# Attention and MLP blocks on one core: residual sums and row statistics moved between engines, another order of the first tiles and of the early weights

## The chip, the cores and the metric

The program runs on one core of a Trainium2 chip, in one launch that holds all four blocks. The metric is the time of one execution on the device in microseconds (us); it is given as a median over executions, with the lowest and the highest.

A core has five engines, each with a queue of its own that is worked off in order: TensorE (PE in the profile; its weight loads are shown apart as PEld), VectorE (DVE), ScalarE (ACT), GpSimd (POOL) and SyncE (SP), which in this kernel issues all the DMAs. Engines wait for each other through semaphores.

## The reference

Two blocks of two kinds alternate: attention, MLP, attention, MLP, over the same rows `x` of 2048 tokens by 576 values, in bfloat16. Before each block the rows are normalized, and each block's output is added to its input. The weights are the same in both rounds.

```python
def _A_ref(x, wqkv, wo):                      # linear attention, 32 heads of 18
    q, k, v = split(x @ wqkv)
    phi = lambda t: jnp.where(t > 0, t + 1, jnp.exp(t)) + 1e-6
    pq, pk = phi(q), phi(k)
    kv = jnp.einsum("bhsd,bhse->bhde", pk, v)
    z = jnp.einsum("bhsd->bhd", pk)
    num = jnp.einsum("bhqd,bhde->bhqe", pq, kv)
    den = jnp.einsum("bhqd,bhd->bhq", pq, z)[..., None] + 1e-6
    return (num / den) @ wo

def _B_ref(x, w1, b1, w2, b2):                # MLP, inner width 4608
    y = _layernorm(x, axis=-1)
    h = _gelu(y @ w1 + b1)
    return h @ w2 + b2

x = x + _A_ref(_layernorm(x), wqkv, wo)
x = x + _B_ref(_layernorm(x), w1, b1, w2, b2)
x = x + _A_ref(_layernorm(x), wqkv, wo)
x = x + _B_ref(_layernorm(x), w1, b1, w2, b2)
```

The MLP normalizes rows that were normalized already. The kernel does both at once: from the variance of a row it forms `u` = var * (1 + eps) + eps^2, and the row is scaled by u^-0.5.

## The kernel before

**Tiles.** The tokens form 16 tiles of 128 rows (tile `t`), one row to a partition, and 4 chunks of 512 tokens (chunk `c`). The 576 columns are split into five blocks of 128 (`KD`), the last of which is half full, or into two halves of 288. The 32 heads lie in five groups `g` of up to seven.

**An attention layer** (`layer_A`) has two stages. In the *key stage* each tile is normalized, turned (transposed into `yT`), and multiplied by the key weights in two halves (`k_half`, L461: half 0 and half 1 of tile t are k(t,0) and k(t,1) below). ScalarE forms an exponential and a shifted copy from each PSUM result, VectorE joins them (`phi_parts`, L393, L396, L400, L404). Then `ky_acc` (L491) accumulates the product of `pk` with the normalized rows over all 16 tiles. Query projections (`q_proj`, L502, 20 of them in a layer, one for each group and chunk) are strewn among the tiles: `q_at` says how many follow each tile, and a list `q_left` gives them out in order. Values need no pass over the tokens: `kv_ps` (L558) multiplies the accumulated product by the value weights, and `kv_wo` (L575) multiplies that by the output weights.

In the *output projection* the denominators of a chunk come from `den_stage` (L590, L598, L600), and `scale_stage` (L606, L608, L609) spreads them over the head columns on TensorE, copies them with ScalarE (`rden_bc`) and multiplies `pq` by them on VectorE. `wo_stage` (L617) then makes the 128x576 output of one tile, in one of two pairs of PSUM banks that take turns: tile t+2 can start when the sum of tile t has been read out. While chunk c is multiplied, chunk c+1 is scaled. After it, `residual` adds the layer's input and stores the rows to DRAM (`x_d`, L448). For tiles 2 and 3 ScalarE copies the PSUM result (L439) and GpSimd adds (L440), for all others VectorE does it in one instruction (L442). The result tile `xn` has five buffers.

**The next norm.** The rows of tiles 0 to 3 go straight on into the MLP's first chunk. `LNPipe` works in steps, one at each `tick`: statistics on VectorE (L278, L279 for the two halves, L284, and `u` in L292), the power on GpSimd (L298), a product (L302), the normalization on GpSimd (L313), and a DMA transpose (L365). For later chunks the MLP loads the rows again from `x_d`.

**The start.** `first_tiles` writes out by hand the order of tiles 0 to 5 on VectorE and ScalarE (`chain_on` binds each instruction to the one before it on its engine). `stats` (L804), `power` (L809, L811 on VectorE, L813 on GpSimd) and `norm` make the normalized rows: tiles 0 to 3 are normalized by VectorE (L820), tiles 4 and 5 by GpSimd (L824, L826). `turn` transposes on TensorE (L836) and copies the result (L839 to L842). From tile 6 on rows come through `LNPipe`, with normalization on GpSimd and a DMA transpose.

**PSUM.** `bank` gives out single banks under two tags, `h` and `g`, of two buffers each, in turn by a counter; once `ky_acc` has taken both buffers of `g`, only `h` is left until the end of the key stage.

**DMA order.** All loads of the start are bound in one chain (`chained`). Later weights (`late_pieces`) are issued between tiles: `piece_count` says how many after which tile, and each is held back until GpSimd's latest normalization (`gate`). The next layer's input rows are fetched ahead of the output projection (`prefetch_xo`, L421).

The MLP (`LayerB`) has two stages per chunk, `h` = gelu of rows times w1 (L718, L714) and the product with w2 (L765), and is not touched.

Of the kernel before, what the change touches and what calls it, by code (L numbers as in the profile page):

```python
# [7 lines left out]
ACT = mybir.ActivationFunctionType  # L8
# [7 lines left out]
P = 128  # L16
# [15 lines left out]
C1 = 1.0 + 1e-6  # L32


def build(tc, A_x, A_wqkv, A_wo, B_w1, B_b1, B_w2, B_b2, out, dbg=None, n_layers=4):
    nc = tc.nc
    dbg = dbg or {}
    with ExitStack() as ctx:
# [5 lines left out]
        bank_turn = dict(n=0, both=True)  # L44
# [133 lines left out]
        load_x0(1)  # L178
        load_wqkv(1, 0)
        load_x0(2)  # L180
        load_wqkv(1, 1)
        load_x0(3)
# [45 lines left out]
        def bias_turn():  # L228
# [6 lines left out]
        late_pieces = [piece_b1_dma, lambda: load_wqkv(2), piece_wo, w1_left[0], w1_left[1], w1_left[2],  # L235
                       lambda: piece_tail(0), w1_left[3], w1_left[4], lambda: piece_tail(1)] + w1_left[5:] + \
                      [(lambda i=i: piece_w2(i)) for i in range(6)]
        piece_count = {4: 1, 5: 2, 6: 1, 7: 2, 8: 1, 9: 1, 12: 2, 14: 3}
# [6 lines left out]
        class LNPipe:  # L245
# [3 lines left out]
            def feed(self, xt, t, kind, norm_eng, evac_eng="dve", load_from=None, after=None, agg_after=None,  # L249
                     keep=False):  # L250
                xbar = evac_eng == "xbar"
                self.items.append(dict(stage=(0 if load_from is None else -1), xt=xt, t=t, kind=kind,
                                       norm=norm_eng, evac=evac_eng, load=load_from,
                                       after=after, xbar=xbar, agg_after=agg_after, keep=keep))
# [4 lines left out]
            def tick(self, transposes=1):  # L259
                for it in list(self.items):  # L260
# [7 lines left out]
                    if st == -1:  # L268
# [5 lines left out]
                        it["xt"] = xn  # L274
                    elif st == 0:
# [20 lines left out]
                    elif st == 1:  # L296
                        rstd = work.tile([P, 1], F32, name="ln_rstd", bufs=6)
                        nc.gpsimd.tensor_tensor(out=rstd[:], in0=it["u"][:], in1=neg_half[:], op=ALU.pow)  # L298
                        it["rstd"] = rstd
                    elif st == 2 and it["norm"] != "dve":  # L300
                        nmr = work.tile([P, 1], F32, name="ln_nmr", bufs=4)
                        nc.gpsimd.tensor_scalar(out=nmr[:], in0=it["mv"][:, 0:1], scalar1=-1.0,  # L302
                                                scalar2=it["rstd"][:, 0:1], op0=ALU.mult, op1=ALU.mult)
                        it["nmr"] = nmr
                    elif st in (2, 3):
                        y = y_ring[state["ycnt"] % NY]
                        state["ycnt"] += 1
# [125 lines left out]
        def residual(li, t, halves, on_pool=False):  # L433
            xo = xo_of.pop((li, t))
            last = (li == n_layers - 1)
            xn = work.tile([P, D], F32, name="xn", tag="xn", bufs=5)
            res = xn[:, 0:HALF].bitcast(BF16) if last else xn[:]
            if on_pool:
                nc.scalar.copy(out=res.rearrange("p (h n) -> p h n", h=2), in_=halves)  # L439
                nc.gpsimd.tensor_tensor(out=res, in0=res, in1=xo, op=ALU.add)  # L440
            else:
                total = nc.vector.tensor_tensor(out=res.rearrange("p (h n) -> p h n", h=2), in0=halves,  # L442
                                                in1=xo.rearrange("p (h n) -> p h n", h=2), op=ALU.add)
                dve_last["sum"] = total.ins.name
            if last:
                nc.sync.dma_start(out=out_f[t * P:(t + 1) * P, :], in_=res)
                return None
            nc.sync.dma_start(out=x_d[t], in_=xn[:])  # L448
            return xn

        def layer_A(li, next_kind, pre_a1=None, first_tiles=None):
# [62 lines left out]
            if li > 0:  # L514
                for t in range(3):
                    y_load(t)
                begin, q_at = 0, {t: 1 for t in range(14)}
            else:
                first_tiles(k_half, ky_acc)
                begin, q_at = 5, {t: 1 + (t in (12, 14)) for t in range(4, NT)}  # L520
                ky_acc(3, range(KD))
                q_proj(*q_left.pop(0))
            for t in range(begin, NT):
                if li > 0 and t + 3 < NT:
                    y_load(t + 3)
                k_proj(t, 0)
                if t in q_at and t >= 1:
                    ky_acc(t - 1, range(KD - 1))
                k_proj(t, 1)
                pre_a1(t)  # L530
                if t >= 1:
                    ky_acc(t - 1, (KD - 1,) if t in q_at else range(KD))
                for _ in range(q_at.get(t, 0)):
                    q_proj(*q_left.pop(0))
# [77 lines left out]
            def wo_stage(t):  # L612
                c, j = divmod(t, TPC)
                wp = ps_acc.tile([P, 2, 512], F32, name="wo_ps", tag=("accA", "accB")[t % 2])
                for half in range(2):
                    for g in range(G):
                        pe(nc.tensor.matmul(wp[:, half, 0:HALF], lhsT=pq[(g, c)][0:GR[g], j * P:(j + 1) * P],  # L617
                                              rhs=kvwo[g][0:GR[g], half * HALF:(half + 1) * HALF],
                                              start=(g == 0), stop=(g == G - 1)))
                xn = residual(li, t, wp[:, :, 0:HALF], on_pool=t in (2, 3))  # L620
                if xn is not None and next_kind == "B" and t < TPC:
                    lnp.feed(xn, t, "B", "pool", "xbar")
# [18 lines left out]
            late_phi(after=dve_last["kvwo"], act_after=act_last["kvwo"])  # L641
            for t in range(NT):
# [3 lines left out]
                wo_stage(t)  # L646
# [9 lines left out]
                if t == NT - 3:  # L656
                    warm_table(ACT.Gelu_apprx_tanh, act_last["copy"])
                lnp.tick()
# [129 lines left out]
        def first_tiles(k_half, ky_acc):  # L788
# [26 lines left out]
            def norm(t, engine):  # L815
# [3 lines left out]
                if engine == "dve":  # L819
                    dve(nc.vector.tensor_scalar(out=y[:, 0:D], in0=it["x"][:], scalar1=it["mv"][:, 0:1],  # L820
                                                scalar2=it["rstd"][:, 0:1], op0=ALU.subtract, op1=ALU.mult))
                else:
                    nmr = work.tile([P, 1], F32, name="ln_nmr", bufs=4)
                    nc.gpsimd.tensor_scalar(out=nmr[:], in0=it["mv"][:, 0:1], scalar1=-1.0,  # L824
                                            scalar2=it["rstd"][:, 0:1], op0=ALU.mult, op1=ALU.mult)
                    last = nc.gpsimd.tensor_scalar(out=y[:, 0:D], in0=it["x"][:], scalar1=it["rstd"][:, 0:1],  # L826
                                                   scalar2=nmr[:], op0=ALU.mult, op1=ALU.add)
                    pool_last["norm"] = last.ins.name
# [23 lines left out]
            norm(0, "dve")  # L852
# [4 lines left out]
            norm(1, "dve")  # L857
            stats(2, (1,))
            power(2)
            a00, d00 = k_half(0, 0)  # L860
            act(*a00())
            turn(1, False)("dve")
            a01, d01 = k_half(0, 1)
            act(*a01())
            norm(2, "dve")
            a10, d10 = k_half(1, 0)
            stats(3)
            turn(2, True)()
            power(3)
            both(d00())  # L870
            act(*a10())
            a11, d11 = k_half(1, 1)
            act(*a11())
            norm(3, "dve")
# [6 lines left out]
            both(d10())  # L881
# [4 lines left out]
            norm(4, "pool")  # L886
            a30, d30 = k_half(3, 0)
            act(*a30())
            both(d20())
            both(d21())  # L890
# [7 lines left out]
            norm(5, "pool")  # L898
            both(d30())
            both(d31())  # L900
# [21 lines left out]
        for _ in range(4):  # L922
            late_pieces.pop(0)()
# [85 lines left out]
```

## Time and profile before

| what | us |
|---|---|
| median of 3 runs | 772.43 (771.15 to 772.85) |
| profiled execution | 770.18 |
| its span, first to last instruction | 768.5 |
| first key matmul (L461) | 6.13 |
| value weights used (L558), first attention layer | 69.32 |
| first output-projection matmul (L617) | 79.00 |
| first MLP matmul (L718) | 106.17 |
| first key matmul of the second attention layer | 388.06 |
| its first output-projection matmul | 456.16 |
| first MLP matmul after it | 483.08 |

A busy share is an average over the span, and the stages differ. The chain of work that ended last, followed back from the last instruction, is 93% TensorE: w2 has 37% of the span, w1 36%, the projections of the two attention layers most of the rest. VectorE has 3% of it, DMA, GpSimd and ScalarE 1% each. In a row of a timeline stand the start, the length (of a merged run of instructions, x their number), the engine, the line, the output and the inputs; in brackets follows how long the engine had been idle and what released it. In a list of waits stand who waited for whom, the total, the number of times and the longest. In a table of stretches each engine has its busy time.

### The profile page before, as it was taken

The numbers are of one execution on the slowest core, as the hardware profiler recorded it, in microseconds if no ns is written. First come the engines' busy times: TensorE is split into PE (matmuls) and PEld (weight loads), VectorE is DVE, ScalarE is ACT, GpSimd is POOL, SyncE is SP. The second block draws the span as 40 slices with busy tenths as digits, with TensorE's granted clock in tenths as the row PEclk, the third lists the DMA queues.
The fourth block names the chain that finished last, engine by engine and source line by source line (L and its number), as shares of the span: only waits on it lengthen the run. The fifth ranks groups of instructions, "written<-read, shape, count | busy, mean of one in ns | idle before, by whom it ended". The sixth has DMA issues, their size and how long they took to land.

```text
span 768.5 us, 15502 instructions
## 1 busy us (share of the span) xinstructions
PE 755.3 (98%) x6402; PEld 480.4 (63%) x6410; DVE 247.3 (32%) x651; ACT 317.9 (41%) x705; POOL 124.0 (16%) x216
## 2 busy tenths in 40 slices
PE   8999899999999999999999999999999999999998
PEld 4766554675477457646776666447745764674476
DVE  7886952125013402301244589462000000000000
ACT  4667546304600750263056674560065026205600
POOL 3670511013000301200100005321010010011000
PEclk9999999999999999999999999999999999999999
DMA  8979584027113703400431039672100110011000
GB/s 246 216 193 334 149 257 96 28 77 148 35 48 97 142 1 81 126 8 17 133 87 47 9 105 262 212 168 71 49 16 2 32 62 1 25 32 39 2 28 20
DMA packets 82865, 71.13 MB, mean 93 GB/s; under 512 B 44970, under 2 KB 67434, under 8 KB 82794
## 3 DMA queue, kind: packets, MB, share of 16 engines
q1 hardware_dynamic: 82794, 70.14, 33.9%
q8 instruction: 50, 0.82, 0.4%
q14 instruction: 21, 0.17, 0.1%
HBM read 41.74 MB, written 18.87 MB: 79 GB/s over the span
## 4 chain that ended last, share of the span: by engine, by line
PE 93%; DVE 3%; DMA 1%; POOL 1%; issue 1%; ACT 1%; SPq 0%; DVEq 0%; POOLq 0%
PE m_ps L765 37%; PE h_ps L718 20%; PE hp_ps L718 16%; PE q_ps L502 5%; PE ky_ps L491 5%; PE k_ps L461 5%; PE wo_ps L617 4%; DVE pq L609 1%; PE rden_ps L606 1%; DMA x_d<-xn 1%; DMA x<-in_A_x_dram 1%; DVE xn L442 0%; PE kv_ps L558 0%; POOL xn L440 0%; DVE kvwo L580 0%
## 5 line engine op out<-in xcount | busy, mean ns | idle before, releaser
L765 PE MATMUL m_ps<-w_sb,hT 128*128 128x288 bf16 x2304 | 283.6, 286 | 0.0
L765 PEld LDWEIGHTS <-hT 128*128 128x128 bf16 x2304 | 224.8, 98 | 59.8 <-issue 3.4
L718 PEld LDWEIGHTS <-w_sb 64*128 64x128 bf16 x2304 | 124.4, 94 | 136.6 <-issue 1.9
L718 PE MATMUL hp_ps<-yT,w_sb 64*128 64x512 bf16 x1152 | 178.0, 376 | 0.0
L442 DVE TENSOR_TENSOR xn<-m_ps,x_ring 128x576 f32<-128x576 f32 (+1 forms) x32 | 24.2, 758 | 415.4 <-PE m_ps L765 415.4
L718 PE MATMUL h_ps<-yT,w_sb 64*128 64x512 bf16 x1152 | 147.9, 376 | 0.0
L723 ACT COPY relay_sb<-relay_sb 128x1 f32<-128x1 f32 x144 | 28.5, 198 | 264.9 <-PE h_ps L718 222.6
L714 ACT ACTIVATE hT<-h_ps,b1T 128x512 bf16<-128x512 f32 x144 | 91.0, 683 | 44.5 <-PE h_ps L718 44.5
L714 ACT ACTIVATE hT<-hp_ps,b1T 128x512 bf16<-128x512 f32 x144 | 91.1, 692 | 0.0
L426 POOL TENSOR_TENSOR x_ring<-x_ring,b_bc 128x576 f32<-128x576 f32 x32 | 40.7, 1275 | 245.8 <-DMA x_ring<-x_d 243.0
L298 POOL TENSOR_TENSOR ln_rstd<-ln_u,neg_half 128x1 f32<-128x1 f32 x58 | 32.4, 559 | 294.1 <-DVE ln_u L289 201.8
L718 PE MATMUL h_ps<-yT,w_tail 64*128 64x512 bf16 x144 | 54.1, 376 | 0.0
L718 PE MATMUL hp_ps<-yT,w_tail 64*128 64x512 bf16 x144 | 54.1, 376 | 0.0
L461 PE MATMUL k_ps<-wqkv_sb,yT 128*128 128x288 bf16 x320 | 49.2, 286 | 0.9 <-ACT phi_a L396 0.6
L491 PE MATMUL ky_ps<-pk,y_ring 128*128 128x192 bf16 (+5 forms) x318 | 48.7, 285 | 0.5 <-ACT phi_a L396 0.2
L502 PE MATMUL q_ps<-yT,wqkv_sb 128*126 128x512 bf16 (+1 forms) x200 | 48.9, 379 | 0.1
L617 PE MATMUL wo_ps<-kvwo,pq 126*128 126x288 bf16 (+1 forms) x320 | 44.1, 286 | 5.0 <-DVE pq L609 3.1
L393 ACT ACTIVATE phi_e<-k_ps 128x288 bf16<-128x288 f32 x64 | 26.5, 413 | 50.9 <-PE k_ps L461 50.6
L617 PEld LDWEIGHTS <-pq 126*128 126x128 bf16 (+1 forms) x320 | 30.1, 97 | 17.8 <-DVE pq L609 5.1
L461 PEld LDWEIGHTS <-yT 128*128 128x128 bf16 x320 | 30.8, 98 | 14.2 <-issue 1.9
L718 PEld LDWEIGHTS <-w_tail 64*128 64x128 bf16 x288 | 27.1, 94 | 17.1
L400 DVE TENSOR_SCALAR phi_e<-phi_e 128x288 bf16<-128x288 bf16 (+2 forms) x104 | 28.5, 274 | 27.1 <-ACT phi_e L393 26.7
(102 smaller groups left out, 482.7 us busy)
## 6 DMA issues: line engine op xcount, KB each, us to landing
x_ring<-x_d SPq DMA_DIRECT2D x66, 288.0 KB, 3.1
x_d<-xn SPq DMA_DIRECT2D x48, 288.0 KB, 2.6
w_sb<-in_B_w_dram SPq DMA_DIRECT2D x6, 864.0 KB, 10.2
w_sb<-in_B_w_dram SPq DMA_DIRECT2D x9, 512.0 KB, 4.8
x<-in_A_x_dram SPq DMA_DIRECT2D x16, 144.0 KB, 3.6
x_ring<-in_A_x_dram SPq DMA_DIRECT2D x16, 144.0 KB, 3.0
y_d<-y_ring SPq DMA_DIRECT2D x16, 144.0 KB, 1.8
y_ring<-y_d SPq DMA_DIRECT2D x16, 144.0 KB, 2.2
```

The costliest lines, as they stand in the source:

```text
L298: nc.gpsimd.tensor_tensor(out=rstd[:], in0=it["u"][:], in1=neg_half[:], op=ALU.pow)
L393: exp = nc.scalar.activation(out=e[0:rows, 0:n], in_=ps_ap, func=ACT.Exp)
L400: low = nc.vector.tensor_scalar(out=e[0:rows, 0:n], in0=e[0:rows, 0:n], scalar1=1.0, scalar2=1e-6, op0=ALU.min, op1=ALU.add)
L426: nc.gpsimd.tensor_tensor(out=xo, in0=xo, in1=b2_bc[:], op=ALU.add)
L461: pe(nc.tensor.matmul(kp[:, 0:HALF], lhsT=yT[:, k, tok], rhs=wqkv_sb[:, k, D + half * HALF: D + (half + 1) * HALF], start=(k == 0), stop=( ...
L491: pe(nc.tensor.matmul(ky[at // 512][:, at % 512:at % 512 + n], lhsT=y_of[t][:, c * P:(c + 1) * P], rhs=pk_tiles[t][:, d:d + n], start=(t = ...
L502: pe(nc.tensor.matmul(qp[0:GR[g], :], lhsT=wqkv_sb[:, k, GO[g]:GO[g] + GR[g]], rhs=yT[:, k, c * CA:(c + 1) * CA], start=(k == 0), stop=(k ...
L617: pe(nc.tensor.matmul(wp[:, half, 0:HALF], lhsT=pq[(g, c)][0:GR[g], j * P:(j + 1) * P], rhs=kvwo[g][0:GR[g], half * HALF:(half + 1) * HALF ...
L714: act_last["gelu"] = nc.scalar.activation(out=hT[f][:, 0:CB], in_=dst[n], func=ACT.Gelu_apprx_tanh, bias=b1T[:, f:f + 1], scale=1.0).ins.name
L718: mm = pe(nc.tensor.matmul(dst[n], lhsT=wt, rhs=mv, start=(seen[n] == 0), stop=(seen[n] == 8)))
L723: relay = nc.scalar.copy(out=relay_sb[:, 1:2], in_=relay_sb[:, 0:1])
L765: pe(nc.tensor.matmul(acc[:, half, 0:HALF], lhsT=hT[f][:, j * P:(j + 1) * P], rhs=w2_sb[:, f, half * HALF:(half + 1) * HALF], start=(f == ...
```

## The change

- **Residual sums.** `residual` has one form again: VectorE adds, for all tiles.
- **Statistics of the MLP's first four tiles.** A new kind, `stat="act"`: ScalarE passes twice over the 576 columns, Identity and Square, each with a running sum over the row; the first sum (scaled) is the second's bias, so that the second sum is the variance. The passes write their unused results into the tile's `y` buffer. `u` moves to GpSimd, and the product's factor takes in the other scale of the mean. These tiles are also handed on one step later: tile t-1 is fed after tile t's work.
- **A query projection** goes from the key stage to a place behind `kv_wo(4)`, ahead of the first output-projection tile. In the first layer tile 13 now has two behind it instead of tiles 12 and 14, in the second layer tile 13 has none.
- **First tiles.** Token tile 2 is loaded ahead of the first half of the key weights, tile 3 ahead of the second half. k(1,0) comes ahead of k(0,1); `power(2)` stands behind the copy of tile 1's transposes; the joins of `phi` move among the norms; tiles 4 and 5 are normalized by VectorE; the bank counter starts at 1.
- **Weights.** Three pieces instead of five are issued before tile 5's work is done. w1's pieces come first; the value weights, the output weights and b1 come after tiles 12 and 13.

```diff
-        bank_turn = dict(n=0, both=True)
+        bank_turn = dict(n=1, both=True)
...
         load_x0(1)
+        load_x0(2)
         load_wqkv(1, 0)
-        load_x0(2)
+        load_x0(3)
         load_wqkv(1, 1)
-        load_x0(3)
...
-        late_pieces = [piece_b1_dma, lambda: load_wqkv(2), piece_wo, w1_left[0], w1_left[1], w1_left[2],
-                       lambda: piece_tail(0), w1_left[3], w1_left[4], lambda: piece_tail(1)] + w1_left[5:] + \
+        late_pieces = w1_left[0:5] + [lambda: piece_tail(0), lambda: piece_tail(1)] + w1_left[5:7] + \
+                      [lambda: load_wqkv(2), piece_wo, piece_b1_dma] + w1_left[7:] + \
                       [(lambda i=i: piece_w2(i)) for i in range(6)]
-        piece_count = {4: 1, 5: 2, 6: 1, 7: 2, 8: 1, 9: 1, 12: 2, 14: 3}
+        piece_count = {4: 1, 5: 1, 6: 1, 7: 2, 8: 1, 9: 1, 12: 2, 13: 1, 14: 3}
...
+                    elif st == 0 and it["stat"] == "act":
+                        xt = it["xt"]
+                        y = it["y"] = y_ring[state["ycnt"] % NY]
+                        state["ycnt"] += 1
+                        mv = work.tile([P, 2], F32, name="ln_mv", bufs=6)
+                        nc.scalar.activation(out=y[:, 0:D], in_=xt[:, 0:D], func=ACT.Identity, scale=-ROOT / D,
+                                             accum_out=mv[:, 0:1])
+                        nc.scalar.activation(out=y[:, 0:D], in_=xt[:, 0:D], func=ACT.Square, scale=ROOT,
+                                             bias=mv[:, 0:1], accum_out=mv[:, 1:2])
+                        it["mv"] = mv
...
                     elif st == 1:
+                        if it["stat"] == "act":
+                            it["u"] = work.tile([P, 1], F32, name="ln_u", bufs=4)
+                            nc.gpsimd.tensor_scalar(out=it["u"][:], in0=it["mv"][:, 1:2], scalar1=1.0 + EPS,
+                                                    scalar2=EPS * EPS, op0=ALU.mult, op1=ALU.add)
...
-        def residual(li, t, halves, on_pool=False):
+        def residual(li, t, halves):
...
-            if on_pool:
-                nc.scalar.copy(out=res.rearrange("p (h n) -> p h n", h=2), in_=halves)
-                nc.gpsimd.tensor_tensor(out=res, in0=res, in1=xo, op=ALU.add)
-            else:
-                total = nc.vector.tensor_tensor(out=res.rearrange("p (h n) -> p h n", h=2), in0=halves,
-                                                in1=xo.rearrange("p (h n) -> p h n", h=2), op=ALU.add)
-                dve_last["sum"] = total.ins.name
+            total = nc.vector.tensor_tensor(out=res.rearrange("p (h n) -> p h n", h=2), in0=halves,
+                                            in1=xo.rearrange("p (h n) -> p h n", h=2), op=ALU.add)
+            dve_last["sum"] = total.ins.name
...
-                begin, q_at = 0, {t: 1 for t in range(14)}
+                begin, q_at = 0, {t: 1 for t in range(13)}
...
-                begin, q_at = 5, {t: 1 + (t in (12, 14)) for t in range(4, NT)}
+                begin, q_at = 5, {t: 1 + (t == 13) for t in range(4, NT)}
...
-                xn = residual(li, t, wp[:, :, 0:HALF], on_pool=t in (2, 3))
-                if xn is not None and next_kind == "B" and t < TPC:
-                    lnp.feed(xn, t, "B", "pool", "xbar")
+                xn = residual(li, t, wp[:, :, 0:HALF])
+                return xn
...
             late_phi(after=dve_last["kvwo"], act_after=act_last["kvwo"])
+            q_proj(*q_left.pop(0))
+            rows_of = {}
             for t in range(NT):
...
-                wo_stage(t)
+                rows_of[t] = wo_stage(t)
...
+                if 1 <= t <= TPC and next_kind == "B":
+                    lnp.feed(rows_of[t - 1], t - 1, "B", "pool", "xbar", stat="act")
                 lnp.tick()
...
             stats(2, (1,))
-            power(2)
             a00, d00 = k_half(0, 0)
             act(*a00())
             turn(1, False)("dve")
+            power(2)
+            both(d00())
+            norm(2)
+            a10, d10 = k_half(1, 0)
+            act(*a10())
+            stats(3, (0,))
             a01, d01 = k_half(0, 1)
+            turn(2, True)()
             act(*a01())
-            norm(2, "dve")
-            a10, d10 = k_half(1, 0)
-            stats(3)
-            turn(2, True)()
+            stats(3, (1,))
             power(3)
-            both(d00())
-            act(*a10())
+            both(d10())
+            norm(3)
...
             power(4)
-            norm(4, "pool")
+            both(d20())
+            norm(4)
+            both(d21())
...
             power(5)
-            norm(5, "pool")
             both(d30())
+            norm(5)
...
-        for _ in range(4):
+        for _ in range(2):
             late_pieces.pop(0)()
```

## The prediction

> **What bounds the kernel now.** First the page's busy times and the list of who waited for whom on TensorE.
>
> ```profile
> PE 755.3 (98%) x6402; PEld 480.4 (63%) x6410; DVE 247.3 (32%) x651; ACT 317.9 (41%) x705; POOL 124.0 (16%) x216
> ```
>
> ```profile
> PE wo_ps L617 <- DVE pq L609: 3.1, 2, 1.6
> PE wo_ps L617 <- DVE kvwo L580: 1.6, 2, 0.8
> ```
>
> TensorE is the bound, at a granted clock of 1.000; the MLP stages are dense. What it waits for lies in two places: the two output projections (3.1 + 1.6 us) and the start. So I read busy time by stretch of the first output projection:
>
> ```profile
> core 0: us, PE busy (x) PEld busy (x) DVE busy (x) ACT busy (x) POOL busy (x), PEclk, DMA share, GB/s
> ...
> 75.00:80.00 5.00, 4.13 (x23) 2.30 (x24) 4.90 (x12) 4.86 (x10) 0.00 (x0) 1.00 0.16 55
> 80.00:85.00 5.00, 4.94 (x56) 3.34 (x56) 4.73 (x12) 2.66 (x6) 0.74 (x2) 1.00 0.38 132
> 85.00:90.00 5.00, 3.43 (x45) 2.17 (x44) 4.90 (x14) 2.16 (x5) 4.73 (x7) 1.00 0.44 136
> 90.00:95.00 5.00, 5.00 (x37) 3.40 (x35) 5.00 (x14) 1.94 (x4) 4.53 (x9) 1.00 0.99 245
> ```
>
> Here VectorE is full (4.7 to 5.0 of 5) and ScalarE mostly free after 80, and TensorE loses most where GpSimd is busy. The timeline of that spot:
>
> ```profile
> 84.61 0.64 ACT L439 COPY xn<-wo_ps 128x576 f32<-128x576 f32 x1 [1.04 <-PE wo_ps L617]
> ...
> 86.43 2.68 POOL L440 TENSOR_TENSOR xn<-xn,x_ring 128x576 f32<-128x576 f32 x2
> 86.67 1.31 DVE L609 TENSOR_TENSOR pq<-pq,rden_bc 72x512 bf16<-72x512 bf16 x1
> ...
> 88.04 0.91 PE L617 MATMUL wo_ps<-kvwo,pq 72*128 72x288 bf16 x6 [1.52 <-DVE pq L609]
> ```
>
> The last scaling of token chunk 1 (L609) takes 1.31 us, where its fellows take 0.42, while GpSimd adds residuals (L440), and TensorE stands 1.52 us for it. The second layer shows the same (1.63 us at 465.31). Last, the start in the chain of work that ended last:
>
> ```profile
> 2.79 3.90 DMA x<-in_A_x_dram
> 6.69 0.02 issue
> 6.71 0.46 DVE ln_st L804
> ...
> 14.82 0.55 POOL ln_rstd L813
> ...
> 15.84 0.83 POOL y_ring L826
> 16.67 0.05 issue
> 16.72 0.45 PE tp L836 x5
> ```
>
> Token tile 2 lands at 6.69, VectorE then works without pause until 14.74, GpSimd's power, product and normalization take until 16.67, and from 16.72 (T4, tile 4's transposes) the chain lies on TensorE alone. T4's time therefore decides the start.
>
> **The change, part by part**, on the clock of the profiled run before.
>
> *First tiles.* Tile 2 is loaded ahead of the first key weights, so VectorE can begin its statistics at 6.05, when tile 0's copy (5.73 + 0.29) is done, instead of 6.71. The key weights (324 KB) now follow 144 KB more: their smaller part landed 3.0 us after its issue at 2.18; I estimate 5.9 to 6.7 for the whole (4.1 us from issue was measured for the second half), so the first k matmul starts at 6.13 to 6.7 and tile 1's transposes run at 7.0 to 7.5. Second comes k(1,0) instead of k(0,1), which needs tile 1's copy: done 7.95 to 8.5. Tile 2's variance comes behind that copy: norm 2 at 9.0 to 9.6 (before 8.97), norm 3 at 11.65 to 12.2 (before 11.28), tile 4's variance at 14.7 to 15.3 (before 14.74). Up to here nothing is won. Then VectorE normalizes tile 4 itself: power 0.55 plus gaps 0.15 (beside a 0.65 of phi work), norm 0.43, T4 at 15.9 to 16.5, because GpSimd's 0.28 + 0.83 fall out. Gain 0.2 to 0.8, taken 0.5. Two norms more on VectorE (0.86) put tile 6's statistics later; its DMA transpose was issued at 22.48, landed 3.1 later at 25.6, and k(6) came at 26.53; now 25.8 to 26.4 against 25.9 to 26.4: that cover is just used up, and fewer weights in the queue ahead of it (1.5 MB for 2.3) help.
>
> *Weights.* The MLP's first weights come before the value weights, the output weights and b1. These are issued near 50 to 54 and land in some 5.5 us (the row of the 576 KB part), by 60; TensorE needs them at 69.3 and 72.6. The w2 loads end 1.05 MB later (near 81 for 78, at the 385 GB/s of 65 to 75), ahead of the first x_d stores at 81.4 and far ahead of their use at 141. Price 0; if that cover went, stores would be late, and the row buffers of the sums behind them (one such wait, 0.96 on VectorE at 102.8).
>
> *One query projection moved* behind kv_wo(4), in each attention layer. No TensorE wait shows from 20 to 66, so the stage it leaves gets shorter by its five matmuls, 1.08. Where it arrives TensorE stood from 78.22 to 79.00, and wo(0) took 1.58 for 1.23. Now the projection runs 78.22 to 79.30, the last scaled rows (79.61) are needed at 79.79, and wo(0) ends at 80.55, as before. Gain 1.08 per layer; 0.78 if only the plain wait counts. Its phi (ScalarE 1.1, VectorE 0.7) stands ahead of the next sums and is in what follows.
>
> *Sums and statistics.* VectorE loses per layer 8 halves of statistics (about 0.42), 4 aggregations (0.20) and 4 small ones (0.15), 4.8 us, and the stretched 0.46 and 0.89 of quad_rden and L609; it gains two sums at 0.75 and the phi of 0.7. GpSimd loses two adds of 1.27 and gains four products of about 0.25. ScalarE loses two copies of 0.64 and gains eight passes over 128x576. Such a pass with a running sum is not in the trace. Nearest below: the copy of that size, 0.64, and gelu 128x512 with a bias, 0.69. Nearest above, far off: GpSimd's 1.275 for that tile. I take 0.70, since it is the same engine and size, plus up to 0.2 (the 128x1 copy, 0.198) for writing the sum.
>
> What waits behind it: the first pass stands in ScalarE's queue ahead of the four copies of chunk 1's denominators, and itself waits for the sum of tile 0 (80.62 to 81.38). So those copies end at 82.6, 83.1, 83.6, 84.1; then Square of tile 0, Identity of tile 1, and the fifth copy at 86.0. VectorE: three scalings to 84.1, reciprocal 85.05, scaling and quad to 85.8, the sum of tile 2 to 86.5 (wo(4) needs its bank), fifth scaling 86.95. wo(4) ends at 87.8, or 88.05 if GpSimd's norm of tile 0 (86.15 to 87.0) holds that scaling; before 88.78. Through chunk 2 alike: wo(8) ends at 94.5, or 95.45 with GpSimd's norms of tiles 1 to 3 in the way of three VectorE operations; before 96.03. Gain 0.58 to 1.55, taken 0.9; in the second layer that point was 0.24 later (473.43 against 456.16 - 79.00 = 377.16), so 1.1. Behind wo(8) TensorE was dense but for some 0.2, and MLP tile 3's transpose, near 96 plus 4.6, is in time for an MLP start near 104.
>
> *The Trainium skill on this.* The row is the 1.31 above; it ended 0.28 after the first GpSimd add. The Trainium skill, SBUF — State Buffer, section "SBUF: two separate sides", has it that a GpSimd operation and a VectorE operation with two SBUF inputs exclude each other for a whole instruction. The trace agrees there. The rule speaks against counting the full gain, as four GpSimd norms remain; what that does is the first rival.
>
> *Sum.* 0.5 + (1.08 + 0.9) + (1.08 + 1.1) = 4.7. The profiled execution took 770.18 (span 768.5, 1.7 around it): 765.5 (span 763.8). The median of the runs is 772.43, 2.25 above the profiled one; less 4.7 this gives 767.7.
>
> **Rivals.**
>
> 1. GpSimd's norms hold VectorE. Four norms of 0.82 stay, and ScalarE's later statistics move them into chunk 2's scalings. For: quad_rden took 0.87 for 0.41 beside the norm at 85.28. Against: those scalings have up to 0.4 of slack. Start 0.2, layers 1.08 + 0.58 and 1.08 + 0.82: gain 3.8, 768.7.
>
> 2. The waits only change place: a pass costs ScalarE about 1.1. Eight stand ahead of chunk 2's last copy (93.0, used at 93.75); eight times 0.4 is 3.2, less 0.75 of slack: 2.45 of the 2.6 that the layer has at best. Gain near 0.8, 771.6. For: ScalarE was 4.86 of 5 busy at 75 to 80. Against: no pass over this size lasts longer than 0.7.
>
> 3. Slower: ScalarE's queue becomes the bound of the output projection. Place: those eight passes, in order ahead of the denominators' copies. From 0.7 + (0.75 + 2.6) / 8 = 1.12 a pass a layer gives back everything; at 1.35, 8 x 0.65 - 3.35 = 1.85 per layer is lost, less 0.5 from the start: +3.2, 775.6. For: each Square needs its Identity's sum, and each copy waits behind both. Against: that is twice any row of its kind.
>
> **How the numbers follow.** Forecast 0.62, rivals 0.20, 0.08, 0.10. The likeliest one's own range goes from 0.8 + 2.6 + 2.8 = 6.2 (766.2) to 3.8 (768.7). With the runs' own spread (771.15 to 772.85) below, and towards rival 2 above, the range is 765.7 to 771.0; some 0.17 lie above and little below. 0.2% is 1.5 us, about what a measurement here can tell from no change: faster 0.62 + 0.20 = 0.82, the same 0.08, slower 0.10.
>
> **What would show it.** Start: T4 between 15.9 and 16.5. Move: no TensorE wait for kvwo, and wo(0) in 1.25. Sums: wo(4) waits under 0.6 for pq, no scaling of 1.3; the passes last 0.7 to 0.9. From first wo matmul to first MLP matmul some 25 us for 27.17 and 26.92. Passes over 1.1, or a value-weight wait near 68, would make it wrong.

## The result and the profile after

| | median us | lowest to highest | executions |
|---|---|---|---|
| before | 772.19 | 771.15 to 772.85 | 4 |
| after | 763.38 | 762.88 to 763.75 | 4 |

The ratio is 0.9887 (95% interval 0.987 to 0.9904): 8.8 us faster, where 4.7 were forecast and 767.7 predicted; 763.38 lies below the range. The profiled execution took 763.75, its span is 762.0 against 768.5. So the two traces differ by 6.5 us, and they show where:

| stretch of the span | before | after | difference |
|---|---|---|---|
| start to tile 4's transposes (T4) | 16.72 | 16.21 | -0.51 |
| T4 to the first value-weight matmul | 52.60 | 51.39 | -1.21 |
| from there to the first MLP matmul | 36.85 | 35.32 | -1.53 |
| second layer: first key matmul to first value-weight matmul | 58.41 | 56.71 | -1.70 |
| from there to the first MLP matmul | 36.61 | 35.09 | -1.52 |
| all the rest | 567.3 | 567.3 | 0.0 |

The page's busy times, then who waited for whom on TensorE:

```profile
PE 755.1 (99%) x6404; PEld 481.5 (63%) x6410; DVE 240.4 (32%) x625; ACT 326.6 (43%) x733; POOL 119.0 (16%) x216
```

```profile
PE warm_ps L196 <- DVE y_ring L189: 1.2, 1, 1.2
PE k_ps L476 <- DVE yT L852: 0.6, 1, 0.6
PE tp L847 <- DVE y_ring L838: 0.4, 2, 0.2
PE wo_ps L633 <- DVE xn L457: 0.3, 2, 0.2
```

TensorE's busy time is the same; what went are its waits. The 3.1 us for `pq` and 1.6 for `kvwo` are gone, and so is one of which the prediction said nothing, in the list of before:

```profile
PE k_ps L461 <- ACT phi_a L396: 0.6, 1, 0.6
```

It stood at 437.42, in the second layer's key stage. The stretches of the first output projection (TensorE, weight loads, VectorE, ScalarE, GpSimd) answer to those shown of before:

```profile
75.00:80.00 5.00, 4.94 (x32) 3.23 (x32) 4.61 (x13) 4.59 (x10) 0.00 (x0) 1.00 1.08 391
80.00:85.00 5.00, 4.81 (x56) 3.27 (x54) 4.81 (x11) 5.00 (x14) 1.45 (x3) 1.00 0.85 302
85.00:90.00 5.00, 5.00 (x57) 3.36 (x56) 4.14 (x8) 4.93 (x13) 4.28 (x9) 1.00 0.90 279
90.00:95.00 5.00, 4.86 (x35) 3.23 (x35) 3.33 (x7) 2.05 (x5) 3.79 (x8) 1.00 0.92 232
```

VectorE was full there and now has room from 85 on; ScalarE is full from 80 to 90 (5.00, 4.93) and free again after; TensorE goes from 3.43 to 5.00 in the stretch from 85. ScalarE's timeline shows what fills it, VectorE's what became of the disputed scaling:

```profile
80.38 2.03 ACT L624 CAST rden_bc<-rden_ps 126x512 bf16<-126x512 f32 x4
82.28 0.80 ACT L283 ACTIVATE y_ring<-xn,ln_mv 128x576 bf16<-128x576 f32 x1
82.96 0.22 ACT L283 ACTIVATION_READ_ACCUMULATOR y_ring<-xn,ln_mv 128x1 f32 x1
83.05 0.69 ACT L281 ACTIVATE y_ring<-xn 128x576 bf16<-128x576 f32 x1
```

```profile
84.44 0.41 DVE L625 TENSOR_TENSOR pq<-pq,rden_bc 72x512 bf16<-72x512 bf16 x1
...
88.35 0.54 DVE L625 TENSOR_TENSOR pq<-pq,rden_bc 126x512 bf16<-126x512 bf16 x1
...
91.19 0.65 DVE L625 TENSOR_TENSOR pq<-pq,rden_bc 72x512 bf16<-72x512 bf16 x1
91.76 0.74 DVE L457 TENSOR_TENSOR xn<-wo_ps,x_ring 128x576 f32<-128x576 f32 x1
94.18 0.76 DVE L457 TENSOR_TENSOR xn<-wo_ps,x_ring 128x576 f32<-128x576 f32 x1 [1.67 <-POOL y_ring L332]
```

The scaling that took 1.31 takes 0.41. Two later ones, beside GpSimd's norms, take 0.54 and 0.65; TensorE waits for neither. In the last row VectorE stands 1.67 us for a GpSimd norm: the sum of tile 8 writes the row buffer of tile 3, which the norm of tile 3 reads until 94.14 (`xn` has five buffers). TensorE's next tile starts at 94.99, 0.05 after that sum. This wait is covered, but only just.

Last the start, in the chain of work that ended last:

```profile
6.20 0.85 PE warm_ps L196 x2
7.05 0.77 PE k_ps L476 x5
...
9.60 0.43 DVE y_ring L838
...
12.16 0.43 DVE y_ring L838
...
15.20 0.98 PE ky_ps L506 x8
16.21 0.45 PE tp L847 x5
```

Tile 2's landing and GpSimd's normalization of tile 4 are gone from it; it runs through the first key matmuls and VectorE's norms of tiles 2 and 3. The row ahead of those matmuls (`warm_ps`, 0.85) is two multiplications without a use, with which the kernel keeps TensorE busy (`warm_pe`, L196); no load is on the chain between them and the key matmuls.

### The profile page after: what moved, and what is told of

It reads as the page before. It is cut to its first block, busy times and chain, and to the rows that moved or that the text cites. A ratio compares the mean times of both kernels' runs of the same rounds, so it can differ in the third digit from the quotient of the medians.

```text
span 762.0 us, 15490 instructions
## 1 busy us (share of the span) xinstructions
PE 755.1 (99%) x6404; PEld 481.5 (63%) x6410; DVE 240.4 (32%) x625; ACT 326.6 (43%) x733; POOL 119.0 (16%) x216
## 4 chain that ended last, share of the span: by engine, by line
PE 96%; DVE 2%; POOL 0%; DMA 0%; issue 0%; ACT 0%; DVEq 0%; POOLq 0%
PE m_ps L784 37%; PE h_ps L737 20%; PE hp_ps L737 16%; PE q_ps L517 6%; PE ky_ps L506 5%; PE k_ps L476 5%; PE wo_ps L633 4%; DVE xn L457 1%; PE rden_ps L622 1%; DVE rden L614 0%; PE kv_ps L574 0%; DVE pq L625 0%; PE den_ps L606 0%; DVE ln_st L823 0%; DMA x<-in_A_x_dram 0%; PE kvwo_ps L591 0%
```

## The experiments

Each is given by its edit, what was expected and what was measured. "Projection" below is the time from the first value-weight matmul to the first MLP matmul, first and second layer: 36.85 and 36.61 before, 35.32 and 35.09 after.

**The kernel before, once more.** No edit.

> The kernel before, unchanged, to see what an ordinary execution of it does. Between the two profiles the span fell by 6.5 us (768.5 to 762.0), between the medians by 8.8. Theory A: the profiled execution of before was a quick one, and the missing 2 us are TensorE waits that it did not have, while other executions do: median 772.2, and a profile of 771 to 773 shows 1.5 to 2.5 us more of such waits than the first, at one place. Theory B: the spread is noise around the span (launch, first loads): the spans agree within 0.5 us and the waits of TensorE are the same.

Measured 770.39 (769.24 to 773.16, 12 executions), beside 770.84 (17 executions of before in the same comparison); ratio 0.9997 (0.9984 to 1.0009). In later comparisons before had medians of 771.18 (32 executions, 769.4 to 775.16) and 771.56 (13). So its median is about 771 (771.1 over all 74), and 772.43, from three, was high. The change is worth some 7.7 us rather than 8.8. Neither theory holds as it stands: the median is not 772.2, and the spans differ by 0.9 (769.4 for 768.5). The trace has that difference in one place, from T4 to the first value-weight matmul (53.43 for 52.60), where tile 6's DMA transpose landed 4.4 us after its issue, for 3.1 in the first profile.

**Weights back.** Order and number of the early weights as before, in the changed kernel.

```diff
-late_pieces = w1_left[0:5] + [lambda: piece_tail(0), ...
+late_pieces = [piece_b1_dma, lambda: load_wqkv(2), piece_wo, w1_left[0], ...
...
-for _ in range(2):
+for _ in range(4):
```

> The changed kernel with the old order and number of early weights. Theory A (weights hidden on both sides): 763.4 to 763.8. Rival W: the early weights (2.3 MB instead of 1.5) delay loads or DMA transposes in the first layer in executions unlike the profiled one, and this is the missing 2 us: about 765.4, with TensorE waits for transposed rows between 20 and 66 us.

Measured 763.72 (763.15 to 763.97), ratio 0.9909 (0.9894 to 0.9924): 0.3 over the changed kernel, which is within the spread of either's four executions, and as Theory A has it. Still, its trace has the one wait that it brings, tile 6's DMA transpose behind the weights:

```profile
PEld L476 <- DMA yT<-y_ring: 1.1, 1, 1.1
```

From T4 to the first value-weight matmul it took 52.04 for 51.39.

**Weights alone**, the same edit the other way round in the kernel before.

> The kernel before with the new order and number of early weights alone. Before ranged from 769.2 to 773.2 over 29 executions, the changed kernel from 762.9 to 763.8 over 4, and one longer execution of before showed the DMA transpose of tile 6 landing 1.3 us later. Theory W: the 2.3 MB of early weights in front of that transpose make the spread; with 1.5 MB the median falls by 0.5 to 1 (769.8 to 770.2) and the spread to 1 to 1.5 us. Rival: the spread has its place elsewhere (stores and transposes in the output projection, whose order against GpSimd's adds varies): spread 3 us or more, median within 0.3.

Measured 769.64 (769.24 to 770.7, 11 executions) beside 771.18; ratio 0.9982 (0.9973 to 0.9991): 1.5 us between the medians. The executions lie closer together (within 1.5 us) than those of before, as Theory W has it, so the early weights probably have a part in its spread. They are not the whole of it: the profiled execution, the longest of these, has no wait for tile 6, but one of 0.96 in the second output projection, behind the store of a row buffer. Both runs point the same way, 0.3 and 1.5 us, where the prediction had none.

**The query projection back**, in the changed kernel; the other placement of `ky_acc` (`apart`) stays.

```diff
-begin, q_at = 0, {t: 1 for t in range(13)}
+begin, q_at = 0, {t: 1 for t in range(14)}
...
-begin, q_at = 5, {t: 1 + (t == 13) for t in range(4, NT)}
+begin, q_at = 5, {t: 1 + (t in (12, 14)) for t in range(4, NT)}
...
-q_proj(*q_left.pop(0))
 rows_of = {}
...
+if li == 0:
+    bank_turn["n"] += 1
```

> The changed kernel with the query projection back in the key stage. Theory A: the gap behind the product of keys, values and output weights comes back: 1.08 in each layer, and 0.5 in the second, where TensorE again waits for a PSUM bank behind tile 13's query projection; 763.4 + 2.6 = 766.0. Rival: the gap is covered otherwise, since ScalarE and VectorE have a phi less ahead of the first sums: 763.4 to 764.6.

Measured 765.38 (765.3 to 765.66), ratio 0.9932 (0.9917 to 0.9947): 2.0 us for the two layers, where Theory A had 2.6. The second key stage takes 57.79, 1.08 over the changed kernel; the projection 35.14 and 34.92, only 0.18 less than with the extra matmuls in it. So 0.90 of the 1.08 is won in the second layer, and the 0.6 wait stays away although the projection is back in its place. In the first layer T4 to the value weights takes 53.06 for 51.39, 1.67 more: besides the 1.08, TensorE stands about 0.4 for one of VectorE's joins at 56.23 and some 0.25 behind a second pair of query projections.

**`apart` alone**, in the kernel before.

```diff
+apart = t - 1 in q_at
-if t in q_at and t >= 1:
+if apart:
...
-ky_acc(t - 1, (KD - 1,) if t in q_at else range(KD))
+ky_acc(t - 1, (KD - 1,) if apart else range(KD))
```

> The kernel before with one line of the diff: whether ky_acc is split between the two key halves is decided by the tile in front (a query projection behind tile t-1 splits tile t). In the second layer the stretch from the first key matmul to the first value-weight matmul was 58.41 before, 57.79 with this rule and the projection in its old place. Theory A: this line alone takes the 0.6 us wait of tile 14 for a PSUM bank away: stretch 57.8, total 0.6 lower than before's. Rival: the wait goes with the other bank parity or the phi order, not with the line: 58.4.

Measured 770.5 (769.55 to 772.26, 10 executions), ratio 0.9994 (0.9983 to 1.0004), which alone decides nothing. The trace does for the stage: 57.79 for 58.41, and no `k_ps` wait in its list. The line that spreads `ky_acc` about the second half now asks whether the tile *before* has a query projection; for tile 14 that keeps TensorE busy until the bank is free. In this execution 0.79 came back later as a wait of the second output projection for a sum, which itself stood for the store of its row buffer:

```profile
481.42 1.46 DVE L442 TENSOR_TENSOR xn<-wo_ps,x_ring 128x576 f32<-128x576 f32 x2 [1.65 <-DMA x_d<-xn]
```

**The query move alone** (with `apart`), in the kernel before.

```diff
+if li == 0:
+    bank_turn["n"] += 1
...
-begin, q_at = 0, {t: 1 for t in range(14)}
+begin, q_at = 0, {t: 1 for t in range(13)}
...
 late_phi(after=dve_last["kvwo"], act_after=act_last["kvwo"])
+q_proj(*q_left.pop(0))
```

> The kernel before with the query move alone (and the line that spreads ky_acc about the second k half, which belongs to it). From the first value-weight matmul to the first MLP matmul it takes 36.85 and 36.61 us before; second layer's key stage 58.41. Theory of the prediction: each layer's key stage shortens by 1.08, and where the projection arrives it lies in a wait that is there anyway, so 36.85 and 36.61 stay within 0.2; with the 0.6 of the bank wait that is 2.8 us in all, some 768.2. Rival: without the other edits the output projection is bound by VectorE's queue, and the projection's phi (0.7 on VectorE) goes ahead of everything in it: 37.5 and 37.3, a gain of 1.4 in all, some 769.6.

Measured 767.28 (766.99 to 767.42) beside 771.56; ratio 0.9946 (0.9932 to 0.9961). The medians differ by 4.3 us, where 2.8 was expected. The span is 765.5, 3.0 below the profile of before: key stages -0.99 (from T4) and -1.70, projection 36.67 and 36.67. The wait for `kvwo` is gone and that for `pq` has barely moved:

```profile
PE wo_ps L620 <- DVE pq L612: 2.9, 2, 1.5
```

The rival, that the projection's phi would delay the scalings by 0.7, fell. So by the traces the query move does what the forecast said, with or without the other edits, and is the largest single part that stands alone. The other 1.3 of the 4.3 lie between the profile of before and its median: these four executions are within 0.4 us of each other, with the early weights as before, and why they lack the spread of before was not shown.

**Statistics back on VectorE**, sums stay there.

```diff
-if 1 <= t <= TPC and next_kind == "B":
-    lnp.feed(rows_of[t - 1], t - 1, "B", "pool", "xbar", stat="act")
+if t < TPC and next_kind == "B":
+    lnp.feed(rows_of[t], t, "B", "pool", "xbar")
```

> The changed kernel with the statistics of the MLP's first four tiles on VectorE again (fed at once, as before); the sums stay on VectorE. Theory A (VectorE bounds the output projection up to chunk 2): 4.8 us of statistics a layer are back in its queue ahead of chunk 1's and 2's scalings, and most of the 1.67 a layer that this stage gained is lost: 766 to 767. Rival L (only the exclusion between GpSimd's adds and VectorE mattered, and these are gone): 763.4 to 764.2.

Measured 765.3 (765.12 to 765.9), ratio 0.9932 (0.9917 to 0.9947). Projection 36.46 and 36.23: 1.14 more in each layer, so most of the gain of this stage is lost, as Theory A has it, though the total is somewhat under its 766. TensorE's wait for `pq` did not come back; it waits for the sum of tile 2 instead, behind the statistics in VectorE's queue:

```profile
PE wo_ps L633 <- DVE xn L457: 2.6, 2, 1.3
```

**Sums alone**, in the kernel before: `on_pool=False` for tiles 2 and 3.

> The kernel before with all residual sums on VectorE, and nothing else. Measured by the stretch from the first value-weight matmul to the first MLP matmul, which is 36.85 (first layer) and 36.61 us (second) before. Theory A: the stretched scalings (0.46 and 0.89) go, two sums of 0.75 come, so VectorE's queue stays as long: 0 to 0.6 a layer gained, most of the gain of this stage is in the statistics. Rival L (the exclusion between GpSimd's adds and VectorE is the main cost): 1.5 or more a layer, total 767.5 or less against 770.7 for before.

Measured 770.81 (769.34 to 771.96, 10 executions), ratio 0.9986 (0.9973 to 0.9999). Projection 36.58 and 36.34: 0.27 a layer, as Theory A has it; Rival L fell. The 3.1 for `pq` left TensorE's list, and 2.8 for `xn` took its place.

**Sums of tiles 2 and 3 back on GpSimd**, statistics stay on ScalarE.

```diff
+if on_pool:
+    nc.scalar.copy(out=res.rearrange("p (h n) -> p h n", h=2), in_=halves)
+    nc.gpsimd.tensor_tensor(out=res, in0=res, in1=xo, op=ALU.add)
```

> The changed kernel with the sums of tiles 2 and 3 on ScalarE and GpSimd again; the statistics stay on ScalarE. Theory A: both GpSimd's adds (2.6 us a layer, holding up VectorE's scalings) and ScalarE's copies come on top of the eight passes: 0.6 to 1.5 a layer lost, 764.6 to 766.4. Rival: with VectorE free of statistics the hold-ups have slack: within 0.5 of 763.4.

Measured 769.59 (768.98 to 771.58, 9 executions), ratio 0.9984 (0.9973 to 0.9995): 6.2 us over the changed kernel, more than expected. Projection 37.71 and 38.56, longer than before the change. ScalarE's timeline in the first layer, and VectorE's and TensorE's behind it:

```profile
86.74 0.68 ACT L281 ACTIVATE y_ring<-xn 128x576 bf16<-128x576 f32 x1 [1.27 <-POOL xn L459]
87.33 0.19 ACT L281 ACTIVATION_READ_ACCUMULATOR y_ring<-xn 128x1 f32 x1
87.42 0.56 ACT L628 CAST rden_bc<-rden_ps 126x512 bf16<-126x512 f32 x1
```

```profile
88.02 0.43 DVE L629 TENSOR_TENSOR pq<-pq,rden_bc 126x512 bf16<-126x512 bf16 x1 [1.62 <-ACT rden_bc L628]
...
89.26 1.40 DVE L629 TENSOR_TENSOR pq<-pq,rden_bc 126x512 bf16<-126x512 bf16 x1
...
90.95 0.74 DVE L461 TENSOR_TENSOR xn<-wo_ps,x_ring 128x576 f32<-128x576 f32 x1
```

```profile
91.75 0.53 PE L637 MATMUL wo_ps<-kvwo,pq 126*128 126x288 bf16 x3 [1.89 <-DVE xn L461]
```

The first statistics pass of tile 2 waits in ScalarE's queue until GpSimd has added that tile. The denominators' copies for chunk 2 stand behind it; VectorE waits 1.62 for one of them, then has a scaling stretched to 1.40 by the next GpSimd add; the sum behind that is late, and TensorE waits 1.89 for its bank. In the kernel before, with statistics on VectorE, the same two additions cost 0.27 a layer. In the second layer the chain is the same (TensorE waits 2.01 at 468.33), and another 0.66 of its loss, at 480.52, is a wait behind the store of a row buffer.

**First tiles back**: loads, order and engines of tiles 0 to 5 as before, in the changed kernel (the diff's hunks on `load_x0`, `norm`, `first_tiles` and the bank counter undone).

> The changed kernel with the loads, the order and the engines of tiles 0 to 5 as before. Theory of the prediction: the start was worth 0.5, so tile 4's transposes come at 16.7 instead of 16.2 and the time is 763.9. Rival: where the key weights land decides the start, in both orders; then T4 stays within 0.2 of 16.2 and the time within 0.3 of 763.4. Second rival: the executions of this order with other weight orders had T4 at 15.4 to 15.7, so 16.2 was a late landing and the start is worth 1.0 to 1.3: 764.5.

Measured 764.61 (764.4 to 764.88), 1.2 over the changed kernel; ratio 0.9913 (0.9898 to 0.9927). Its T4, 16.22, is as in the changed kernel's profile, but the first value-weight matmul comes at 68.07 for 67.60. One profile of each is not enough here, since T4 varies. Seven traces with the changed start have it at 15.41 to 15.72 (six) and 16.21 (the changed kernel's own profile), median 15.63; seven with the old start have it at 16.22 to 16.80, median 16.66. Four variants with the changed start, and with the projection and the weights as changed, reach the value weights at 66.73 to 66.96.

In the changed start T4 follows the first key matmul: 6.17 and 15.41, 6.39 and 15.63, 6.55 and 15.72, in the changed kernel's own profile 6.84 and 16.21. The landing of the key weights, which both rivals of this run name, is not what moves it: with a first key matmul at 6.18 (statistics back on VectorE) these loads landed 3.9 to 4.2 us after their issue, as they did with 6.84. The chain that ended last is the same in both executions, two transposes, three more and the two multiplications of `warm_pe`, all on TensorE, and TensorE is slower at them. In the changed kernel's profile they take 0.40, 0.32 and 0.85, in the kernel with a third ScalarE pass (the next experiment) 0.28, 0.17 and 0.43:

```profile
5.90 0.43 PE warm_ps L196 x2
```

The granted clock reads 1.00 in both. Why TensorE's first matmuls take up to twice as long in some executions stays open. So the first rival has its T4 by chance, but not its time, and the second rival's number holds, though not its reason: the profile of the changed kernel caught a slow start of TensorE, and the start is worth about 1.0 (between the medians of T4) to 1.2 (between the medians of the runs).

**A third ScalarE pass** for each of the four tiles.

```diff
+nc.scalar.activation(out=y[:, 0:D], in_=xt[:, 0:D], func=ACT.Identity, scale=-ROOT / D,
+                     accum_out=mv[:, 1:2])
 nc.scalar.activation(out=y[:, 0:D], in_=xt[:, 0:D], func=ACT.Identity, scale=-ROOT / D,
                      accum_out=mv[:, 0:1])
```

> The changed kernel with a third ScalarE pass (Identity with running sum) for each of the four tiles, 0.79 each, 3.2 us per layer; the results stay what they were. Queue theory (third rival of the prediction: slack 0.75 a layer, the rest shows): 2.4 a layer, some 768.2, with TensorE waiting for pq. Rival: ScalarE stands idle 2.26 + 0.59 us behind the passes in chunk 2, so only the wait in chunk 1 appears (1.1 a layer): 765.6. If the queue has nothing to do with the end: 763.4.

Measured 765.92 (765.86 to 766.17), ratio 0.993 (0.9914 to 0.9947). Projection 36.82 and 36.59: 1.50 a layer for 3.2 of work, between the two figures and nearer the lower. The wait is the one that the prediction's third rival named:

```profile
PE wo_ps L635 <- DVE pq L627: 2.2, 4, 0.7
```

So ScalarE's queue would have become the bound; the actual passes, 0.69 and 0.80, stay below that point.

**A GpSimd addition more** ahead of each of the four norms; the norm overwrites its result.

```diff
+nc.gpsimd.tensor_tensor(out=it["y"][:, 0:D], in0=it["xt"][:, 0:D], in1=it["xt"][:, 0:D], op=ALU.add)
```

> The changed kernel with one GpSimd addition of two 128x576 operands more in front of each of the four MLP norms (1.27 each, its result is overwritten by the norm); nothing else runs longer. Hold-up theory (first rival of the prediction): such an addition stretched a scaling from 0.42 to 1.31 before, so with four of them at least one scaling or sum a chunk is stretched by 0.9 in time that TensorE needs: 1 to 2 us a layer, 765.4 to 767.4. Rival: VectorE has slack in that stretch now, single scalings are stretched but TensorE's waits stay under 0.3: 763.4 to 763.9.

Measured 770.83 (770.51 to 772.41, 10 executions), ratio 0.9995 (0.9986 to 1.0005): all of the gain is gone. Projection 38.47 and 39.64, 3.15 and 4.55 longer, more than either side expected. VectorE's timeline of the first layer:

```profile
90.67 0.76 DVE L459 TENSOR_TENSOR xn<-wo_ps,x_ring 128x576 f32<-128x576 f32 x1 [0.57 <-POOL y_ring L334]
91.35 1.37 DVE L627 TENSOR_TENSOR pq<-pq,rden_bc 72x512 bf16<-72x512 bf16 x1
94.46 0.76 DVE L459 TENSOR_TENSOR xn<-wo_ps,x_ring 128x576 f32<-128x576 f32 x1 [1.74 <-POOL y_ring L334]
```

and TensorE's list:

```profile
PE wo_ps L635 <- DVE xn L459: 6.0, 8, 1.8
PE wo_ps L635 <- DVE pq L627: 1.3, 2, 0.6
```

The scaling is stretched to 1.37, as the hold-up theory has it, but that is the smaller part (1.3 us of waits). The larger one, 6.0, is the covered wait of the changed kernel laid open: sums stand until a GpSimd norm frees the row buffer of five tiles earlier. The first of those norms was itself held up; it takes 1.32 for 0.82, beside two of VectorE's scalings that ran unstretched (0.74 for the two, from 89.37):

```profile
89.32 1.32 POOL L334 TENSOR_SCALAR y_ring<-xn,ln_rstd,ln_nmr 128x576 bf16<-128x576 f32 x1
```

A sixth row buffer would be the direct test; no run has it.

## Why the prediction was wrong

It had the sign and most of the mechanisms. The base, the sizes of the start and of the sums and statistics, and two terms that it put at nothing (a bank wait, the weights) were off.

**Base: wrong.** The last step subtracts the gain from 772.43. The kernel's executions spread from 769.2 to 775.2 with a median of 771.1 (74 of them), so the forecast of 4.7 us amounts to 766.4. Of the miss of 4.3 (767.7 against 763.4) that is 1.3; the rest, 3.0, is the gain, forecast as 4.7 where some 7.7 are measured. What makes the kernel before spread isn't settled: two waits come and go between profiles of before and its close variants, tile 6's DMA transpose (0.7 in the second profile of before) and the row store shown above (0.79 with `apart` alone, 0.96 with the weights alone), and whether they are all of it was not shown.

**Sums and statistics: term mis-sized**, 0.9 and 1.1 where the runs give 1.35 and 1.58 (query move alone against the changed kernel, which also differ in start and weights, but not in this stage). The step that failed is the discount for GpSimd's norms holding VectorE. Worked without it, the step put the end of the ninth tile's multiplication at 94.5 on before's clock; measured is 92.81 + 1.58 = 94.39. With it, 95.45. The norms do hold scalings up (0.54 and 0.65 for 0.42), but VectorE then waits for something else anyway, and TensorE for neither. That a scaling is held until the GpSimd instruction is over, as the Trainium skill has it (SBUF — State Buffer, section "SBUF: two separate sides": the two take turns for whole instructions), agrees with these rows. What was wrong was to price a held instruction as if it lay on the path. The slack of up to 0.4 that the first rival counted against itself was enough.

**And it is one term, not two.** The four combinations, by projection: neither 36.67 and 36.67; sums alone 36.46 and 36.23; statistics alone 37.71 and 38.56; both 35.32 and 35.09. Alone the one gains 0.2 to 0.4 and the other loses 1.0 and 1.9 (0.66 of the latter is the wait behind a store); together they gain 1.35 and 1.58. The prediction summed both engines' loads and so had the pair in one term, but nothing in it says that half of the change would have been a loss.

**The bank wait in the second key stage: not counted**, 0.62. The prediction's "No TensorE wait shows from 20 to 66" was read in the first layer and applied to both; the list of waits of before had the 0.6 for `k_ps`. The `apart` line, which removes it, was passed over as part of the query move.

**Query projection: right.** 1.08 a layer was taken; alone it gives 0.99 + 0.18 and 1.08 - 0.06, in the changed kernel 1.49 in the first layer (1.67 less 0.18) and 0.90 in the second. The wait for `kvwo` is gone. wo(0) took 1.28 in the chain of work that ended last, near the 1.25 of the forecast; in the timeline, where an undisturbed tile takes 1.40, it went from 1.58 to 1.44.

**Start: size low, and one step wrong.** T4 at 16.21 is within 15.9 to 16.5 by luck: that execution had a slow start of TensorE, and the six others of that order are at 15.41 to 15.72, below the range. The step that failed is VectorE's working between the norms. For a first key matmul at 6.13 the prediction had norm 2 at 9.0, norm 3 at 11.65, tile 4's variance at 14.7 and T4 at 15.9; with that matmul at 6.17 (third-pass kernel) they came at 8.80, 11.36, 14.26 and 15.41. The four stretches were counted 0.24, 0.09, 0.15 and 0.05 too long. So "Up to here nothing is won" doesn't hold: 0.48 is won by tile 4's variance (14.26 for 14.74), and GpSimd's part falling out comes on top.

**Weights: price 0 was off by 0.3 to 1.5 in favour.** The trace with the weights back shows where: tile 6's transpose queues behind them (1.1). The prediction named that cover ("just used up") but priced only its loss.

**Rivals.** The first (norms hold VectorE, 768.7) is not what happened, though it was near: with four additions more, 4.7 us of GpSimd work a layer, the gain is gone, mostly by the row buffers, which no rival named. The second and third failed on their condition: a pass takes 0.69 or 0.80 and the sum's own instruction 0.19 to 0.22, mostly beside the next, under the 1.12 of break-even. Dosed, they are real, with 1.50 a layer for 3.2 us.

The parts, from medians and traces, nearly add up: start 1.0 to 1.2, query 2.0 to 2.4, bank wait 0.6, sums and statistics 2.9, weights 0.3 or more, together 6.8 to 7.4 or more of some 7.7; the rest is within the spread of before.

## What to carry to other kernels

When an instruction is stretched by another engine, follow who waits for it before pricing the stretch: 0.65 for 0.42 cost nothing here, and taking away the 1.31 alone won 0.27 of the 1.52 that TensorE stood for it, because the next sum in VectorE's queue was as late. When two edits move work between the same engines, price each without the other as well: here one alone was a loss because it put a queue behind an engine that the other edit had freed. Measure the base more than three times before a change of one per cent is sized against it. And before a late start is put down to a load, read in the chain what released it, in more than one trace: here T4 differed by 0.8 between executions of the same order.

## What the runs showed of the hardware

- A ScalarE pass with a running sum is two instructions: the pass (0.69 Identity, 0.78 to 0.80 Square, 128x576) and an `ACTIVATION_READ_ACCUMULATOR` of 0.19 to 0.22. The next instruction starts about 0.1 after the latter began: from the start of a pass to the start of what follows its sum it is 0.67 to 0.78, or 0.80 to 0.82 where an Identity is followed by its own Square, which needs the sum.
- A VectorE multiplication with two operands in on-chip memory that starts while a GpSimd instruction over 128x576 runs ended, in these rows, 0.27 to 0.28 after it: 88.89 after 88.62 and 91.84 after 91.57 in the changed kernel, 92.72 after 92.45 with more additions, 90.66 after 90.38 with the sums on GpSimd. It can go the other way: with more additions a norm at 89.32 took 1.32 for 0.82, while two multiplications beside it ran at full speed. Sums that read one operand from PSUM ran on beside the norms at 0.74 to 0.76.
- TensorE's first matmuls take up to twice as long in some executions as in others at a granted clock of 1.00: two multiplications of `warm_pe` took 0.43 in one and 0.85 in another. The first key matmul of the changed start came at 6.17 to 6.84 by that, and T4 at 15.41 to 16.21 with it.
